# Fourth row tiles behind branches replaced by pieces of 32 rows, four at a time on four column tiles

## The chip, the core and the metric

The kernel runs on one core of a Trainium2 chip. The metric is the device time of one execution in microseconds (us), lower is better. The engines are named as in the profile: PE is TensorE's matmuls, PEld its weight loads, DVE is VectorE, ACT is ScalarE, POOL is GpSimd and SP is SyncE, which issues most of the DMAs.

## What is computed

A gated linear recurrence over 768 steps for 4 x 8 heads of 48 channels, and behind it a mixture of eight experts: each of the 3072 tokens goes through the two matrices of the one expert that its logits name.

```python
f = 1.0 / (1.0 + np.exp(-f_logit))
for t in range(S):                                   # S = 768
    state = f[:, :, t, :, None] * state + np.einsum('bhd,bhe->bhde', k[:, :, t], v[:, :, t])
    y[:, :, t] = np.einsum('bhd,bhde->bhe', q[:, :, t], state)
x = y.transpose(0, 2, 1, 3).reshape(3072, 384)
...
expert_idx = np.argmax(x @ w_gate, axis=1)           # 8 experts
for e in range(E):
    h = np.maximum(x_sorted[lo:hi] @ w1[e], 0.0)     # w1[e]: 384 x 1024
    y_sorted[lo:hi] = h @ w2[e]                      # w2[e]: 1024 x 384
return gate_w[:, None] * y_sorted[inv_perm]
```

Everything is float32. How many rows an expert gets depends on the data; counted from the reference's inputs they are 406, 413, 352, 385, 335, 443, 396 and 342.

## The kernel before

The first part works through 12 units of the recurrence in a software pipeline (`score`, `within`, `before`, `added`, `rows`) and scatters each token's row of 400 numbers (`xrow`: 384 channels, the token's number, its gate weight, filling) to the tensor `xs` in HBM, where each expert has a region of its own.

The second part takes the rows of one expert in tiles of 128. For a tile, `load_rows` fetches the rows (SP), `turn` transposes them on PE (three transposes into `etp`, one DVE copy to `xT`), `widen` multiplies by `w1` (24 matmuls of 128 columns into `hps`, then one ReLU on ACT and one on DVE into `hT`), and `narrow` multiplies by `w2` (8 matmuls of 384 columns into `yps`), scales by the gate weight (`ysb`, DVE) and scatters to the output (POOL). Each matmul of float32 stands in the profile as two MATMUL records with two weight loads.

A list `order` names the tiles: four per expert (`TILES = 4`), without the first tile of experts 0 and 1, which run earlier, inside the pipeline of the first part (`soon`). Engines run it in the order in which it is written. Row loads run some tiles ahead and turns two tiles ahead (`ahead`), from seven row buffers (`rowp`). The weights of expert e + 2 (3 MB) are loaded when the last tile of expert e is done, since `wpool` holds two experts.

The fourth tile of each expert stands behind a branch, which each engine takes or not by a register that it loads from `endi` (L664, L682); it is executed for the five experts with more than 384 rows. A second branch (L684) guards a loop for rows past the fourth tile, which no expert here has. The transposes of a fourth tile are made whether it is executed or not. `check` (L620 on) sums a test of the recurrence's range and sets `fixi`; at the end of the program a branch on it leads to a slow path that does the work again.

Of the kernel before, what the change touches and what calls it, by code (L numbers as in the profile page):

```python
# [34 lines left out]

REGION = N + C
ROWS = E * REGION


TILES = 4  # L40


EARLY = 2
# [12 lines left out]
def _consts():  # L56
    p = np.arange(128)
    e = np.arange(E)

    def row(v):  # L60
        return np.broadcast_to(v, (128, len(v)))

    f = {
        "ident": np.eye(128),
        "tri": np.triu(np.ones((128, 128)), 1),
        "ones": np.ones((128, 128)),
        "rev": row(E - e),
        "first": row(e * REGION),
        "full": row(e * REGION + C),
        "tok": p[:, None] + np.arange(N // C)[None] * C,  # L70
        "p": p[:, None],
        "sel": np.stack([p < DP, p >= DP], 1),
    }
# [26 lines left out]
def kernel(  # L100
# [24 lines left out]
    def const(name):  # L125
        a, w = fat[name]
        return fpack[:, a : a + w]
# [1 line left out]
    causal = mpack[:, 0:128]  # L129
    ident = const("ident")  # L130

    xs = nc.dram_tensor("xs", (ROWS, ROW), F32, kind="Internal").ap()
    xg = nc.dram_tensor("xg", (B, DM, S), F32, kind="Internal").ap()

    badi = cpool.tile([1, 1], I32, name="badi")
# [127 lines left out]
    def narrow(x, w, yp, group="out"):  # L263
        for f in range(NF):
            nc.tensor.matmul(  # L265
                yp, lhsT=x["hT"][:, f, :], rhs=w[1][:, f, :], start=f == 0, stop=f == NF - 1
            )
        ysb = ep.tile([128, DM], F32, name="ysb")
        nc.vector.tensor_scalar(ysb, yp, x["x"][:, GATE : GATE + 1], None, op0=OP.mult)  # L269
        scatter(out, x["dst"], ysb, N - 1, group)  # L270
# [6 lines left out]
    redo = cpool.tile([1, 1], I32, name="redo")  # L277
    fix = cpool.tile([1, 1], F32, name="fix")
    fixi = cpool.tile([1, 1], I32, name="fixi")
    endi = cpool.tile([1, E], I32, name="endi")  # L280

    def load_weights(e):
        w1t = wpool.tile([128, KD, F], F32, name="w1t")
# [14 lines left out]
        done[what] = max(done[what], min(count, len(order)))  # L298

    def load_pads(e):  # L300
        rows = xs[e * REGION : e * REGION + TILES * C]
        nc.sync.dma_start(
            rows.rearrange("(t p) r -> p t r", p=C), _bc(pad, 1, TILES)
        )

    with ExitStack() as st:
        ld = st.enter_context(tc.tile_pool(name="ld", bufs=4))
# [236 lines left out]
        for n in range(NU + 2):  # L544
# [33 lines left out]
            if rt:  # L578
                rt.place()
                rt.fill()  # L580
                lead["base"] = rt.after
                if n == NU - 3:
                    lack = wk.tile([1, EARLY], F32, name="lack", bufs=1)
                    some = wk.tile([1, 1], F32, name="some", bufs=1)
                    nc.vector.tensor_tensor(
                        lack, rt.after[0:1, 0:EARLY], const("full")[0:1, 0:EARLY], op=OP.is_lt
                    )
                    nc.vector.reduce_max(some, lack, axis=AX_X)
                    nc.vector.tensor_copy(redo, some)
# [29 lines left out]
                soon = [load_rows(slice(first[e], first[e] + C)) for e in range(EARLY)]  # L619


        def check():
# [11 lines left out]
            nc.vector.tensor_tensor(fix, fix, bad[0:1], op=OP.max)  # L634
            nc.vector.tensor_copy(fixi, fix)
            nc.vector.tensor_copy(endi, lead["base"][0:1])
# [10 lines left out]
    def tile_pools(st):  # L647
        pool = lambda name, bufs: st.enter_context(tc.tile_pool(name=name, bufs=bufs, space=PSUM))
        psh, pse, psz = pool("psh", 4), pool("pse", 2), pool("psz", 2)

        def turn_late(x):
            turn(x, pse.tile([128, KD, C], F32, name="etp"))

        def through(x, w, between=(), group="out"):
            hp = [psh.tile([128, 4, C], F32, tag="hps", name="hps") for g in range(2)]
            widen(x, w, hp, range(NF))
            for y in between:
                turn_late(y)
            narrow(x, w, psz.tile([128, DM], F32, name="yps"), group)

        return turn_late, through

    def rows_end(e):
        return nc.values_load(endi[0:1, e : e + 1], min_val=first[e], max_val=first[e] + N)  # L664

    def rows_from(row, e, rows_to, w, turn_late, through, group="out"):

        nc.sync.dma_start(xs[ds(rows_to, C)], pad)
        with tc.For_i(row, first[e] + N, C) as at:
            with tc.If(rows_to > at):  # L670
                x = load_rows(at)
                turn_late(x)
                through(x, w, group=group)

    with ExitStack() as st:
        turn_late, through = tile_pools(st)
        st.enter_context(tc.manual_schedule(engines=ordered))
        for i, (e, t) in enumerate(order):
            w = weights[e]
            if t == TILES - 1:  # L680
                rows_to = rows_end(e)
                with tc.If(rows_to > first[e] + t * C):  # L682
                    through(tiles[e, t], w)
                    with tc.If(rows_to > first[e] + TILES * C):  # L684
                        rows_from(first[e] + TILES * C, e, rows_to, w, turn_late, through)
                if e + 2 < E:
                    load_weights(e + 2)
                continue

            more = 1 if t == TILES - 2 else 0  # L690
            list(ahead("load", i + 6 + more))
            through(tiles[e, t], w, list(ahead("turn", i + 3 + more)))

    todo = nc.values_load(fixi[0:1, 0:1], min_val=0, max_val=1)
    with tc.If(todo > 0):

        again = nc.values_load(redo[0:1, 0:1], min_val=0, max_val=1)
        with tc.If(again > 0):
            with ExitStack() as st:
                turn_late, through = tile_pools(st)  # L700
                for e in range(EARLY):
                    load_weights(e)
                    x = load_rows(slice(first[e], first[e] + C))
                    turn_late(x)
                    through(x, weights[e], group=None)


        flag = nc.values_load(badi[0:1, 0:1], min_val=0, max_val=1)
        with tc.If(flag > 0):
            with ExitStack() as st:  # L710
# [73 lines left out]
            with ExitStack() as st:  # L784
                turn_late, through = tile_pools(st)
                for e in range(E):
                    load_weights(e)
                    rows_from(first[e], e, rows_end(e), weights[e], turn_late, through, group=None)


_OUTS = [((N, DM), "float32")]
# [53 lines left out]
```

## Time and profile before

| | us |
|---|---|
| median of 3 runs (494.04 to 496.79) | 496.4 |
| the profiled execution, its own time | 494.94 |
| its span, first to last instruction | 493.1 |
| PE busy (share of the span) | 443.6 (90%) |
| DVE busy | 161.5 (33%) |
| ACT busy | 124.4 (25%) |
| POOL busy | 117.3 (24%) |

The time of an execution is 1.8 us more than its span. A busy PE is a PE with at least one matmul in flight. The granted clock, 0.972 of TensorE's full 2.4 GHz over the span, is its mean.

### The profile page before, as it was taken

The page shows a single profiled execution, that of the slowest core. Times are in us where ns is not written, and L with a number is a line of the kernel's source. Part 1 is how long each engine was busy: PE and PEld are TensorE (multiplying, and loading weights), DVE is VectorE, ACT ScalarE, POOL GpSimd, SP SyncE. Part 2 cuts the span into 40 slices and gives each one's busy share as a digit, 9 for nine tenths or more (in the row PEclk, how much of TensorE's full clock was granted, in tenths as well). Part 3 has the DMA queues.
Part 4 walks back from the last instruction along what each step waited for, and adds up shares of the span by engine and source line. Part 5 has one row for each costly group of instructions (what it writes and reads, how often), then busy time and mean ns, then how long its engine had stood idle before and what let it go on. Part 6 is the DMA issues. An engine that isn't in the chain of part 4 may idle for free.

```text
span 493.1 us, 8760 instructions
## 1 busy us (share of the span) xinstructions
PE 443.6 (90%) x3678; PEld 367.2 (74%) x3678; DVE 161.5 (33%) x326; ACT 124.4 (25%) x172; POOL 117.3 (24%) x135
## 2 busy tenths in 40 slices
PE   0498898898989999999999999999999999999990
PEld 0497797797988778777788788777778878877770
DVE  5787667778543212111111111211111111121110
ACT  5788487977732000000000000000000000000000
POOL 4656466765623200000001000000000100000000
PEclk9889799998999999999999999999999999999995
DMA  8999865799221411062081271053181127000000
GB/s 316 409 384 383 322 235 218 277 397 347 92 102 68 145 37 34 17 230 98 17 293 48 71 285 33 18 209 114 35 298 36 33 86 262 19 17 5 16 20 17
DMA packets 31858, 74.49 MB, mean 151 GB/s; under 512 B 3358, under 2 KB 19777, under 8 KB 31792
## 3 DMA queue, kind: packets, MB, share of 16 engines
q1 hardware_dynamic: 27696, 63.49, 35.6%
q0 software_dynamic: 3392, 9.64, 5.1%
q8 instruction: 38, 0.62, 0.5%
q10 hardware_dynamic: 704, 0.51, 0.3%
q14 instruction: 28, 0.23, 0.1%
HBM read 57.44 MB, written 17.17 MB: 151 GB/s over the span
## 4 chain that ended last, share of the span: by engine, by line
issue 53%; PE 30%; ACT 6%; POOL 4%; DVE 2%; another core or an unknown queue 1%; POOLq 1%; DMA 1%; ACTq 0%
PE s L391 5%; PE xp L496 5%; PE yt L435 4%; POOL out_dram L149 3%; PE dp L451 3%; PE yt L415 2%; PE hps L251 2%; PE yp L265 2%; PE yps L265 2%; PE s L251 2%; ACT L371 2%; PE kp L406 2%; ACT f L371 1%; ACT f L340 1%
## 5 line engine op out<-in xcount | busy, mean ns | idle before, releaser
L251 PEld LDWEIGHTS hps<-xT,w1t 128*128 128x128 f32 x1296 | 148.4, 192 | 14.7 <-PEq L684 4.2
L251 PE MATMUL hps<-xT,w1t 128*128 128x128 f32 x1296 | 149.6, 275 | 5.3 <-DVEq L684 2.4
L265 PE MATMUL yps<-w2t,hT 128*128 128x384 f32 x432 | 143.8, 486 | 0.0
L265 PEld LDWEIGHTS yps<-w2t,hT 128*128 128x128 f32 x432 | 80.0, 190 | 50.1
L149 POOL DMA_INDIRECT out_dram<-ysb,dst x29 | 28.1, 969 | 289.0 <-DVE ysb L269 209.0
L259 ACT ACTIVATE hT<-hps 128x512 f32<-128x512 f32 x27 | 16.1, 597 | 285.6 <-PE hps L251 285.6
L261 DVE TENSOR_SCALAR hT<-hps 128x512 f32<-128x512 f32 x27 | 18.7, 692 | 136.0 <-PE hps L251 136.0
L269 DVE TENSOR_SCALAR ysb<-yps,xrow 128x384 f32<-128x384 f32 x27 | 16.7, 618 | 114.1 <-PE yps L265 114.1
L391 PE MATMUL s<-q,k 64*128 64x128 f32 x384 | 28.1, 303 | 15.1 <-POOL last L374 15.1
L391 PEld LDWEIGHTS s<-q,k 64*128 64x128 f32 x384 | 25.8, 212 | 15.9 <-POOL last L374 15.1
L348 DVE TENSOR_TENSOR_SCAN r<-f,cap 128x1032 f32<-128x1032 f32 (+1 forms) x13 | 28.7, 2208 | 12.4 <-POOL f L341 12.4
L394 DVE COPY_PREDICATED at<-mpack,s 128x1024 f32<-128x1024 uint8 x24 | 30.2, 1311 | 4.4 <-PE s L391 4.4
L149 POOL DMA_INDIRECT xs<-xr,posi x24 | 24.2, 1007 | 24.3 <-DVE xr L220 7.5
L360 POOL TENSOR_TENSOR k<-k,r 128x1024 f32<-128x1024 f32 (+1 forms) x13 | 26.4, 2032 | 2.5 <-DVE r L348 2.4
L496 PE MATMUL xp<-fpack,ys 128*128 128x104 f32 x192 | 24.3, 280 | 0.7 <-ACT ys L476 0.7
L496 PEld LDWEIGHTS xp<-fpack,ys 128*128 128x128 f32 x192 | 22.3, 191 | 2.2 <-ACT ys L476 1.0
L415 PE MATMUL yt<-at,v 128*64 128x128 f32 x384 | 23.6, 276 | 0.0
L435 PE MATMUL yt<-q,state 48*48 48x128 f32 x320 | 22.5, 297 | 0.0
L415 PEld LDWEIGHTS yt<-at,v 128*64 128x64 f32 x384 | 20.7, 137 | 1.2
L435 PEld LDWEIGHTS yt<-q,state 48*48 48x48 f32 x320 | 19.5, 133 | 2.1 <-issue 1.8
L379 DVE TENSOR_TENSOR q<-q,f 128x1024 f32<-128x1024 f32 (+1 forms) x13 | 14.8, 1145 | 15.0 <-ACT f L371 12.7
L406 PE MATMUL kp<-fpack,k 128*128 128x128 f32 x96 | 14.4, 286 | 5.7 <-ACT kn L407 3.9
(75 smaller groups left out, 325.5 us busy)
## 6 DMA issues: line engine op xcount, KB each, us to landing
w1t<-in_moe_w_dram SPq DMA_DIRECT2D x8, 1536.0 KB
w2t<-in_moe_w_dram SPq DMA_DIRECT2D x8, 1536.0 KB
xs<-pad SPq DMA_DIRECT2D x8, 800.0 KB
xrow<-xs SPq DMA_DIRECT2D x32, 200.0 KB
v<-in_vu_dram SPq DMA_DIRECT2D x12, 512.0 KB
f<-in_fu_dram SPq DMA_DIRECT2D x11, 516.0 KB
k<-in_ku_dram SPq DMA_DIRECT2D x11, 512.0 KB
q<-in_qu_dram SPq DMA_DIRECT2D x11, 512.0 KB
```

What stands on the lines that cost most here:

```text
L149: ins = nc.gpsimd.indirect_dma_start(out=dst, out_offset=bass.IndirectOffsetOnAxis(ap=idx, axis=0), in_=src, in_offset=None, bounds_check= ...
L251: nc.tensor.matmul(hp[g][:, f, :], lhsT=w[0][:, j, b * 128 : b * 128 + 128], rhs=x["xT"][:, j, :], start=j == 0, stop=j == KD - 1,)
L261: nc.vector.tensor_scalar(x["hT"][:, 4:8], hp[1], 0.0, None, op0=OP.max)
L265: nc.tensor.matmul(yp, lhsT=x["hT"][:, f, :], rhs=w[1][:, f, :], start=f == 0, stop=f == NF - 1)
L348: nc.vector.tensor_tensor_scan(x["r"][:, part].rearrange("p s c -> p (s c)"), x["f"][:, part].rearrange("p s c -> p (s c)"), cap[:, part]. ...
L360: nc.gpsimd.tensor_tensor(k, k, r[:, :, 1:CR], op=OP.mult)
L391: nc.tensor.matmul(ps[:, h, p], lhsT=x["k"][r, s], rhs=x["q"][r, s], start=True, stop=True)
L394: nc.vector.copy_predicated(x["at"][:, a].rearrange("p h s c -> p (h s) c"), _bc(causal, 1, SEG), ps.rearrange("p h s c -> p (h s) c"),)
L406: nc.tensor.transpose(kp[:, p], x["k"][:, HP * a + p], ident)
L415: nc.tensor.matmul(x["yt"][r, a, p], lhsT=x["v"][:, a, 2 * p + h], rhs=x["at"][:, a, h, p], start=p == 0, stop=x["old"] is None, skip_grou ...
L435: nc.tensor.matmul(x["yt"][r, a, p], lhsT=x["old"][r, HP * a + p], rhs=x["q"][r, HP * a + p], start=False, stop=True, skip_group_check=True,)
L496: nc.tensor.matmul(xp[:, p], lhsT=x["ys"][:, a, p], rhs=wx[:, p], start=True, stop=True)
```

## The change

`TILES` becomes 3: an expert's first 384 rows run as before, without a branch. Rows behind them are cut into pieces of 32, at most four per expert and eight in all (`SPILL`, `SLOTS`). `share` works out on DVE, from the experts' counts, which piece stands in which of the eight slots, and leaves for each slot the row in `xs` and the expert in `sloti`; an empty slot names a block of padding rows (`NONE`) and expert 0. For the inputs here six slots are filled.

A quad is four slots. `load_quad` reads eight registers on SP and issues twelve DMAs: 32 rows per slot, and `w1` and `w2` of each slot's expert, 3 MB per slot and 12.6 MB per quad, into a pool with one buffer (`qp`). On PE the rows of the four slots are turned together; then `widen_quad` takes each slot's 32 rows of `xT` as the stationary operand, so that the product fills 32 of the array's columns, with the slot's own `w1` as the moving operand of 512 columns. The four slots write to four groups of 32 partitions of the same bank. `turn_quad` transposes the 1024 hidden values of each row back (8 transposes) and `narrow_quad` multiplies by `w2` in the same way, 384 columns at a time.

Quad 0 is loaded ahead of the list of 22 tiles and runs in its tile number 11 (counted from 0), quad 1 is loaded behind that tile and runs in the last, number 21. Row buffers go from seven to six, and rows are loaded four tiles ahead. `check` moves behind the early `widen` of expert 1. The slow path is written anew; the branch on `fixi` that leads to it stays.

```diff
-TILES = 4
+NONE = ROWS
+TILES = 3
+T = 32
+QUADS = 2
+SLOTS = 4 * QUADS
+SPILL = 4
+PADDED = TILES * C + SPILL * T
...
-    rowp = ctx.enter_context(tc.tile_pool(name="rowp", bufs=7))
+    rowp = ctx.enter_context(tc.tile_pool(name="rowp", bufs=6))
...
+        def share():
...
+            nc.vector.tensor_tensor(flat, flat, rank, op=OP.mult)
+            nc.vector.tensor_tensor(
+                mine,
+                _bc(flat, 1, SLOTS),
+                _bc(const("slots")[one], 2, E * SPILL),
+                op=OP.is_equal,
+            )
...
         list(ahead("load", 5))
+        over = share()
         narrow_early(soon[0], weights[0])
-        check()
         widen(soon[1], weights[1], early_banks(), range(NF))
+        check(over)
...
+        qp = st.enter_context(tc.tile_pool(name="qp", bufs=1))
...
+        def load_quad(q):
+            x = qp.tile([128, ROW], F32, name="qrow")
+            w1 = qp.tile([128, 4, KD, F], F32, name="qw1")
+            w2 = qp.tile([128, 4, NF, DM], F32, name="qw2")
...
+            for g in range(4):
+                nc.sync.dma_start(x[g * T : g * T + T], xs[ds(value(0, g, NONE), T)])
+            for g in range(4):
+                e = value(1, g, E - 1)
+                for w, src, k in ((w1, moe_w1, KD), (w2, moe_w2, NF)):
+                    nc.sync.dma_start(
+                        w[:, g], src[ds(e, 1)].rearrange("o (k p) f -> p (o k) f", p=128)
+                    )
...
+        def widen_quad(x):
+            hp = banks()
+            hq = qp.tile([128, 2, 4, C], F32, name="hq")
+            for b in range(2):
+                for j in range(KD):
+                    for g, r in pieces():
+                        nc.tensor.matmul(
+                            hp[b][r].rearrange("p f c -> p (f c)"),
+                            lhsT=x["xT"][:, j, r],
+                            rhs=x["w"][0][:, g, j, b * 512 : b * 512 + 512],
...
+        def narrow_quad(x):
+            yp = psz.tile([128, DM], F32, name="yps")
+            for f in range(NF):
+                for g, r in pieces():
+                    nc.tensor.matmul(
+                        yp[r],
+                        lhsT=x["hT"][:, f, r],
+                        rhs=x["w"][1][:, g, f],
...
+        quads = {len(order) // 2: 0, len(order) - 1: 1}
+        quad = load_quad(0)
         for i, (e, t) in enumerate(order):
             w = weights[e]
-            if t == TILES - 1:
-                rows_to = rows_end(e)
-                with tc.If(rows_to > first[e] + t * C):
-                    through(tiles[e, t], w)
...
-            list(ahead("load", i + 6 + more))
-            through(tiles[e, t], w, list(ahead("turn", i + 3 + more)))
+            list(ahead("load", i + 5))
+            if i in quads:
+                turn_late(quad)
+                widen_quad(quad)
+            hp = banks()
+            widen(tiles[e, t], w, hp, range(NF))
+            if i in quads:
+                turn_quad(quad)
+            for x in ahead("turn", i + 3):
+                turn_late(x)
+            narrow_late(tiles[e, t], w)
+            if i in quads:
+                narrow_quad(quad)
+                if quads[i] + 1 < QUADS:
+                    quad = load_quad(quads[i] + 1)
+            if t == TILES - 1 and e + 2 < E:
+                load_weights(e + 2)
```

On PE, this is what stands around the fourth tile of expert 0 in the kernel before (`etp` are turns, `hps` is `widen`, `yps` is `narrow`; L682 and L684 are the two branches, the rows between L669 and L670 the loop that is skipped here).

```order
L265 MATMUL yps<-w2t,hT 128x384 x8
L664 TENSOR_LOAD endi
L682 COMPARE_AND_BRANCH
L251 MATMUL hps<-xT,w1t 128x128 x24
L265 MATMUL yps<-w2t,hT 128x384 x8
L684 COMPARE_AND_BRANCH
L669 COMPARE_AND_BRANCH
L669 UNCONDITIONAL_BRANCH x2
```

In the changed kernel no branch is left between the tiles. This is PE around tile 11 and quad 0 (`qrow`, `qw`, `hq` and `hqT` belong to the quad, `32x512` and `32x384` are the outputs of its matmuls).

```order
L277 MATMUL yps<-w2t,hT 128x384 x8
L250 MATMUL etp<-fpack,qrow 128x128 x3
L770 MATMUL hps<-qw_2020,xT 32x512 x24
L263 MATMUL hps<-xT,w1t 128x128 x24
L789 MATMUL hps<-fpack,hq 128x128 x8
L250 MATMUL etp<-fpack,xrow 128x128 x3
L277 MATMUL yps<-w2t,hT 128x384 x8
L798 MATMUL yps<-qw_2021,hqT 32x384 x32
```

The tile's own `widen` now lies between the quad's `widen` and the turning back of its result; the quad's own turn is followed at once by the product that needs it.

On SP, before, two or three row loads followed a load of weights, with the branches behind them:

```order
L284 DMA w1t<-in_moe_w_dram 128x3x1024
L286 DMA w2t<-in_moe_w_dram 128x8x384
L232 DMA xrow<-xs 128x400 x3
L664 TENSOR_LOAD endi
L664 ISA x2
L682 COMPARE_AND_BRANCH
L684 COMPARE_AND_BRANCH
```

In the changed kernel this is the end of the load of quad 1 (its last slot's expert) and what follows it on the same queue; the first `xrow` is the row load of tile 16, issued at the head of tile 12, and the `w1t` and `w2t` are those of expert 6.

```order
L748 TENSOR_LOAD sloti
L748 ISA x2
L755 ISA
L755 DMA qw_2853<-in_moe_w_dram 128x3x1024
L755 ISA
L755 DMA qw_2854<-in_moe_w_dram 128x8x384
L244 DMA xrow<-xs 128x400
L300 DMA w1t<-in_moe_w_dram 128x3x1024
L302 DMA w2t<-in_moe_w_dram 128x8x384
```

Tile 16's rows, which PE turns in tile 14, now stand on SP behind the 12.6 MB of the quad.

## Rows read from the trace of the kernel before

**Rows 1.** The page: busy time of PE, and GB/s in 40 slices of the span.
```profile
PE 443.6 (90%) x3678; PEld 367.2 (74%) x3678; DVE 161.5 (33%) x326; ACT 124.4 (25%) x172; POOL 117.3 (24%) x135
...
GB/s 316 409 384 383 322 235 218 277 397 347 92 102 68 145 37 34 17 230 98 17 293 48 71 285 33 18 209 114 35 298 36 33 86 262 19 17 5 16 20 17
```

**Rows 2.** PE in order of time (start, length, engine, line, xcount, idle before).
```profile
224.29 5.52 PE L251 MATMUL hps<-xT,w1t 128*128 128x128 f32 x48
229.65 0.82 PE L238 MATMUL etp<-fpack,xrow 128*128 128x128 f32 x6
230.30 5.33 PE L265 MATMUL yps<-w2t,hT 128*128 128x384 f32 x16
235.47 5.52 PE L251 MATMUL hps<-xT,w1t 128*128 128x128 f32 x48
240.82 5.33 PE L265 MATMUL yps<-w2t,hT 128*128 128x384 f32 x16
246.79 5.59 PE L251 MATMUL hps<-xT,w1t 128*128 128x128 f32 x48 [0.64 <-PEq L684]
```

**Rows 3.** The first and last tile of the list, in order of time.
```profile
180.12 5.52 PE L251 MATMUL hps<-xT,w1t 128*128 128x128 f32 x48
...
475.09 5.33 PE L265 MATMUL yps<-w2t,hT 128*128 128x384 f32 x16
...
480.46 0.62 DVE L269 TENSOR_SCALAR ysb<-yps,xrow 128x384 f32<-128x384 f32 x1 [4.41 <-PE yps L265]
```

**Rows 4.** Groups of line 415: xcount, busy us, mean ns of one, idle before.
```profile
L415 PE MATMUL yt<-at,v 128*64 128x128 f32 x384 | 23.6, 276 | 0.0
L415 PEld LDWEIGHTS yt<-at,v 128*64 128x64 f32 x384 | 20.7, 137 | 1.2
```

**Rows 5.** PE around one group of line 415, in order of time.
```profile
106.18 1.97 PE L415 MATMUL yt<-at,v 128*64 128x128 f32 x32
108.07 1.09 PE L406 MATMUL kp<-fpack,k 128*128 128x128 f32 x8
```

**Rows 6.** The copy behind a turn on DVE, in order of time.
```profile
174.23 0.55 DVE L240 COPY xT<-etp 128x384 f32<-128x384 f32 x1
```

**Rows 7.** SP's issues, in order of time.
```profile
212.95 0.38 SPq L284 DMA_DIRECT2D w1t<-in_moe_w_dram  x1
213.42 0.43 SPq L286 DMA_DIRECT2D w2t<-in_moe_w_dram  x1
213.95 11.52 SPq L232 DMA_DIRECT2D xrow<-xs  x3
```

**Rows 8.** SP's DMA queue from 212.9 to 222.9, then to 224.2: packets, MB, share.
```profile
q1 hardware_dynamic: 1437, 3.16, 89.6%
...
q1 hardware_dynamic: 287, 0.39, 84.6%
```

**Rows 9.** Register loads on SP by line: ns min/median/max, first and last start.
```profile
L664 SPq TENSOR_LOAD <-endi x8: 266/270/662, 192.2 to 417.1; - x8
L664 SPq FUSED_REGOPS  x8: 147/154/159, 192.5 to 417.8; - x8
```

**Rows 10.** PE after an idle stretch early in the run and, last, undisturbed.
```profile
23.92 1.95 PE L451 MATMUL dp<-v,kn 128*64 128x48 f32 x32 [4.21 <-ACT kn L407]
25.80 3.35 PE L391 MATMUL s<-q,k 64*128 64x128 f32 x32
...
32.31 1.16 PE L451 MATMUL dp<-v,kn 128*64 128x48 f32 x32 [0.24 <-ACT kn L407]
33.40 2.06 PE L391 MATMUL s<-q,k 64*128 64x128 f32 x32
```

**Rows 11.** Two windows of 2 us: busy by engine, then the granted clock.
```profile
24.00:26.00 2.00, 2.00 (x34) 1.91 (x36) 1.19 (x1) 1.64 (x2) 0.78 (x1) 0.50 1.02 380
...
30.00:32.00 2.00, 2.00 (x28) 1.66 (x24) 1.78 (x2) 1.86 (x3) 2.00 (x4) 1.00 1.05 365
```

**Rows 12.** PE at the check, in order of time.
```profile
167.77 0.35 PE L630 MATMUL op<-okc,fpack 128*128 128x1 f32 x2 [1.21 <-DVE okc L628]
```

More of the change, by code (lines that the diff above doesn't have):

```diff
@@ L69, in _consts @@
         "full": row(e * REGION + C),
+        "most": row(e * REGION + PADDED),
+        "spill": row((e[:, None] * REGION + TILES * C + np.arange(SPILL) * T).ravel()),
+        "spillat": row((e[:, None] * REGION + TILES * C + np.arange(SPILL) * T).ravel() - NONE),
+        "spillof": row(np.repeat(e, SPILL)),
+        "slots": row(1 + np.arange(SLOTS)),
         "tok": p[:, None] + np.arange(N // C)[None] * C,
@@ L267, in narrow, with put @@
             )
+        put(x, yp, group)
+    def put(x, yp, group):
         ysb = ep.tile([128, DM], F32, name="ysb")
@@ L619 @@
                 soon = [load_rows(slice(first[e], first[e] + C)) for e in range(EARLY)]
-        def check():
+        def share():
+            one = slice(0, 1)
+            have = wk.tile([1, E, SPILL], F32, name="have", bufs=1)
+            rank = wk.tile([1, E * SPILL], F32, name="rank", bufs=1)
+            mine, part = (
+                cap[0:1].rearrange("p s c -> p (s c)")[:, i : i + SLOTS * E * SPILL].rearrange(
+                    "p (s e) -> p s e", s=SLOTS
+                )
+                for i in (0, SLOTS * E * SPILL)
+            )
+            slot = wk.tile([1, SLOTS], F32, name="slot", bufs=1)
+            over = wk.tile([1, E], F32, name="over", bufs=1)
+            flat = have.rearrange("p e s -> p (e s)")
+            ends = lead["base"][one]
+            nc.vector.tensor_tensor(
+                have,
+                _bc(ends, 2, SPILL),
+                const("spill")[one].rearrange("p (e s) -> p e s", e=E),
+                op=OP.is_gt,
+            )
+            nc.vector.tensor_tensor_scan(
+                rank, const("ones")[one, 0 : E * SPILL], flat, 0.0, OP.mult, OP.add
+            )
+            nc.vector.tensor_tensor(flat, flat, rank, op=OP.mult)
+            nc.vector.tensor_tensor(
+                mine,
+                _bc(flat, 1, SLOTS),
+                _bc(const("slots")[one], 2, E * SPILL),
+                op=OP.is_equal,
+            )
+            with nc.allow_low_precision("whole numbers"):
+                nc.vector.tensor_tensor(
+                    part, mine, _bc(const("spillat")[one], 1, SLOTS), op=OP.mult
+                )
+                nc.vector.reduce_sum(slot, part, axis=AX_X)
+                nc.vector.tensor_scalar(sloti[:, 0], slot, float(NONE), None, op0=OP.add)
+                nc.vector.tensor_tensor(
+                    part, mine, _bc(const("spillof")[one], 1, SLOTS), op=OP.mult
+                )
+                nc.vector.reduce_sum(sloti[:, 1], part, axis=AX_X)
+            nc.vector.tensor_tensor(over, ends, const("most")[one], op=OP.is_gt)
+            nc.vector.reduce_max(slot[:, 0:1], over, axis=AX_X)
+            nc.vector.tensor_scalar(
+                slot[:, 1:2], rank[:, E * SPILL - 1 :], SLOTS + 0.5, None, op0=OP.is_gt
+            )
+            nc.vector.tensor_tensor(slot[:, 0:1], slot[:, 0:1], slot[:, 1:2], op=OP.max)
+            nc.vector.tensor_copy(endi, ends)
+            return slot[:, 0:1]
@@ L623, in check @@
+        def check(over):
             ok = wk.tile([128, NU * SEG], F32, name="ok", bufs=1)
@@ L649, in tile_pools, with banks @@
         psh, pse, psz = pool("psh", 4), pool("pse", 2), pool("psz", 2)
+        def banks():
+            return [psh.tile([128, 4, C], F32, tag="hps", name="hps") for g in range(2)]
         def turn_late(x):
             turn(x, pse.tile([128, KD, C], F32, name="etp"))
[L654 to L658, printed above, removed]
-            narrow(x, w, psz.tile([128, DM], F32, name="yps"), group)
@@ L661, in tile_pools, with narrow_late @@
[L661 to L673, printed above, removed]
+        def narrow_late(x, w, group="out"):
+            narrow(x, w, psz.tile([128, DM], F32, name="yps"), group)
@@ new lines, in pieces @@
+        def pieces():
+            return [(g, slice(g * T, g * T + T)) for g in range(4)]
+        def widen_quad(x):
[8 more added lines that the diff above has]
+                            rhs=x["w"][0][:, g, j, b * 512 : b * 512 + 512],
+                            start=j == 0,
+                            stop=j == KD - 1,
+                            skip_group_check=True,
+                        )
+                if b == 0:
+                    nc.scalar.activation(hq[:, b], hp[b], AF.Relu)
+                else:
+                    nc.vector.tensor_scalar(hq[:, b], hp[b], 0.0, None, op0=OP.max)
+            x["hq"] = hq
@@ new lines, in turn_quad @@
+        def turn_quad(x):
+            tp = banks()
+            x["hT"] = qp.tile([128, NF, C], F32, name="hqT")
+            for b in range(2):
+                for f in range(4):
+                    nc.tensor.transpose(tp[b][:, f], x["hq"][:, b, f], ident)
+                (nc.scalar.copy if b == 0 else nc.vector.tensor_copy)(
+                    x["hT"][:, 4 * b : 4 * b + 4], tp[b]
+                )
+        def narrow_quad(x):
[6 more added lines that the diff above has]
+                        rhs=x["w"][1][:, g, f],
+                        start=f == 0,
+                        stop=f == NF - 1,
+                        skip_group_check=True,
+                    )
+            put(x, yp, "out")
@@ L694 @@
+            narrow_late(tiles[e, t], w)
[5 more added lines that the diff above has]
+                load_weights(e + 2)
     todo = nc.values_load(fixi[0:1, 0:1], min_val=0, max_val=1)
     with tc.If(todo > 0):
[L697 to L705, printed above, removed]
@@ L783 @@
                 nc.vector.tensor_copy(endi, end[0:1])
[L784 to L788, printed above, removed]
+        skip = nc.values_load(fromi[0:1, 0:1], min_val=0, max_val=TILES * C)
+        with ExitStack() as st:
+            banks, turn_late, narrow_late, psz = tile_pools(st)
+            with tc.For_i(0, E) as e:
+                w1t = wpool.tile([128, KD, F], F32, name="w1t")
+                w2t = wpool.tile([128, NF, DM], F32, name="w2t")
+                for w, src in ((w1t, moe_w1), (w2t, moe_w2)):
+                    nc.sync.dma_start(
+                        w, src[ds(e, 1)].rearrange("o (k p) f -> p (o k) f", p=128)
+                    )
+                rows_to = nc.values_load(
+                    endi[0:1, ds(e, 1)], min_val=0, max_val=ROWS - C
+                )
+                nc.sync.dma_start(xs[ds(rows_to, C)], pad)
+                with tc.For_i(e * REGION + skip, rows_to, C) as at:
+                    x = load_rows(at)
+                    turn_late(x)
+                    widen(x, (w1t, w2t), banks(), range(NF))
+                    narrow_late(x, (w1t, w2t), None)
 _OUTS = [((N, DM), "float32")]
```

31 lines of the change are left out of this document (18 added, 13 removed).

## The prediction

> **What bounds the kernel now.** I began with the page. PE is busy for 90% of the span, and in the later half of it the DMA engines move 5 to 300 GB/s where they moved 383 to 409 in the second to fourth slice [rows 1]: up to about 170 us the recurrence and the transfers matter, behind that PE alone. Then I read PE in order of time there. One tile follows the next: from the start of one `widen` to that of the next it is 235.47 - 224.29 = 11.18 us, of which `widen` is 5.36, two turns 0.65 and `narrow` 5.17 [rows 2]. So a tile costs 10.53 us and a turn 0.33 us. Of `narrow` that is 16 records of 384 columns at 0.323 us each. The next start, past a skipped or taken branch, is 246.79 - 235.47 = 11.32 us, 0.80 more than a tile without turns [rows 2]. The list runs from 180.12 to 480.26 (0.2 us ahead of the last `ysb`), which is 300.1 us [rows 3]: 27 tiles at 10.53 are 284.3, 28 turns are 9.2, and 6.6 are left for the branches of eight experts, 0.8 each, as the one seen. Behind it lie 12.8 us of the last scatter and the end of the program, which stay. What counts is what PE does between 180 and 480 us, and whether something makes it wait there.
>
> **What is removed.** Five fourth tiles (experts 0, 1, 3, 5, 6) of 10.53 us, 52.7. Eight turns, 2.6. The branches, 6.6. Together 61.9 us.
>
> **What two quads cost on PE.** Each turn of a quad stands right ahead of the product that needs it, so PE waits for the copy: the DVE first writes `ysb` of the tile before (0.2 us behind, 0.62 long [rows 3]), then copies for 0.55 [rows 6], so the product starts about 1.45 us after the turn starts. The products are 24 matmuls of 512 columns and 32 of 384, two records each. If the four slots run at once, there are 12 steps of 0.323 x 512/384 = 0.43 us and 16 of 0.323: 5.2 + 5.2 us. If they run one after another, it is four times that, 41.4 us a quad. The trace has no group of four, but it has groups of two: line 415 fills 64 columns with each matmul, and two that follow each other write different halves. Its 32 records take 108.07 - 106.18 = 1.89 us [rows 5], 0.118 us for two of 128 columns, where `widen` needs 5.36 / 48 = 0.112 for one. Two streams therefore cost what one costs. The weight load of such a record takes 0.137 us [rows 4], longer than the step, so loads lie beside matmuls too. I take four at once, since two show no loss. The same group took 0.1 us more than 16 steps of 0.112, which I read as the price of going from whole-array to divided matmuls; four such changes a quad are 0.4 at most. Eight transposes back are 0.9. ReLU and copies of the quad lie beside the tile's own `widen` and `narrow`, which are written between; without that cover they would cost about a microsecond each. A quad is 1.45 + 10.4 + 0.9 + 0.4 = 13.1 us, two are 26.2.
>
> The Trainium skill, "TensorE: Matmul & The Clock Gate", Part 3 (Measured speedup vs the span model), gives three column tiles of 512 columns a speedup of 2.38, not 3. By that the products would take 10.4 x 3 / 2.38 = 13.1 us, and the sum would be 5 us higher; line 415 shows no such loss with two.
>
> **What moves at the start of the list.** PE's wait of 1.21 us for `okc` [rows 12] goes, since `check` stands behind `widen` of expert 1 now; there `okc` waits for that tile's ReLU and holds up the two turns, which cost about 0.6 again. `share`'s fourteen small DVE operations lie under `narrow` of expert 0, 5 us long, which needs nothing from the DVE meanwhile. -0.6 us.
>
> **What the transfers do.** A quad's 12.6 MB go through the one queue on which all row loads stand. How that queue serves is seen where weights are loaded: `w1t` and `w2t` are issued at 212.95 and 213.42, and row loads (0.2 MB each) from 213.95 on [rows 7]. Until 222.9 the queue moved 3.16 MB, the size of the weights; the next 1.3 us moved 0.39 MB, the two row loads [rows 8]. They came last, in the order of issue, though their issue was 9 us old. So whatever is issued behind a quad's weights lands behind them.
>
> Quad 0 is issued as soon as `check` has freed the memory, at about 176 us. Its four registers and row loads come first: 0.27 + 0.15 us for a register [rows 9] and 0.4 for an issue, some 4.5 us. 12.6 MB at 0.39 MB/us (the busy slices of [rows 1]) are 32 us, so with about a microsecond each to start and to land, and the output's scatters, it is in by 216. Tile 5's rows are behind it and are turned in tile 3, at 179.5 + 3 x 10.86 + 5.36 = 217.4: just hidden. Expert 2's weights follow by 221 and 225 and are needed from 223 (`w1`) and 228 (`w2`). Cost nothing, with 2 us to spare; the tiles 0 to 4 are the cover.
>
> Quad 1 is not hidden. It is issued when `ysb` of quad 0 is written, 0.85 us after PE has left quad 0 (call that E). Weights are issued from E + 4.5, the bytes are through at about E + 38, with the scatters of three tiles at E + 39. Tile 16's row load is issued behind them, at the head of tile 12, and lands at about E + 40.3. PE turns these rows in tile 14, between its `widen` and `narrow`: E + 2 x 10.86 + 5.36 = E + 27.1. PE waits 13 us, and `narrow` of tile 14 is queued behind the turn, so nothing else fills it. Bounds: at the fastest slice, 0.409 MB/us, the wait is 11.6 us; if each expert took the 9.95 us of [rows 7, 8] with its start, 20.7. I take 13, since eight weight loads in a row need one start only. Behind it expert 6's weights (by E + 49) and tile 17's rows are in time, for the wait has moved PE too.
>
> After such an idle stretch PE is slow: 4.21 us of it, and the next two groups took 1.95 and 3.35 us where they otherwise take 1.16 and 2.06 [rows 10], at a granted clock of 0.50, the level of 1.2 GHz, against 1.00 later [rows 11]. That is 2.1 us more; I add 2.
>
> **The sum.** The profiled execution took 494.9: a span of 493.1 and 1.8 around it, 1.5 below the median of 496.4. 494.9 - 61.9 + 26.2 - 0.6 + 15 = 473.6. I say 474.
>
> **The rivals.**
> (1) No wait at tile 14: 474 - 15 = 459. It needs row loads that pass the weights, or a quad that is in 13 us sooner. [Rows 8] speak against the first, the slices against the second.
> (2) Two slots at a time. Line 415 has two halves only, so a limit of two would look the same there. Each quad costs 10.4 us more: 495, no change.
> (3) The slower side: slots one after another, or loads of stationary rows that no longer hide. The first gives 474 + 2 x 31 = 536. For the second the nearest row is 0.137 us a load [rows 4]; 112 loads a quad in the open are 15.3 us, 30.7 in all, 505. What decides is the time of a step of four slots: the change loses from 2.1 times a single stream on, since a quad may cost (496.4 - 474) / 2 = 11 us more. Against it stand [rows 4, 5], where streams and loads of two column groups on the same rows of the array lie beside each other. The Trainium skill, "TensorE: Matmul & The Clock Gate", Part 3 (The mechanism), says that a weight load overlaps a running matmul only when the row group differs; by that rule the second of these would come. Line 415's column groups share all rows and its loads overlap, so the trace disagrees.
> (4) Quad 0 late too: if SP's registers or the bytes take 5 us more than I reckon, tile 3 and expert 2 wait 3 to 7 us: 477 to 481.
>
> **How the numbers follow.** The forecast 0.64 (470 to 481 with its bounds), rival 1 0.14, rival 2 0.09, rival 3 0.07, rival 4 0.06. The range 456 to 486 takes in the forecast, 1 and 4, and a loss of a quarter in the products; it leaves out 2 and 3, 0.16. A measurement here can tell 0.5% from no change, 2.5 us: rival 2 straddles that bound, 0.07 of it same, 0.02 faster. Faster 0.64 + 0.14 + 0.06 + 0.02 = 0.86, same 0.07, slower 0.07.
>
> **What the profile after would show.** 22 pairs of `hps` and `yps` groups and nothing between them but turns; MATMUL records of 32 x 512 that begin in fours, and 48 of them in about 5.2 us; a group of 64 with 384 columns in as long; one wait of PE of about 13 us with a row load as its end, about 27 us behind quad 0, and a granted clock of 0.5 behind it; DMA at 390 GB/s for 33 us twice. If the quad's groups take 10 or 20 us, the step on the four streams is wrong; if the wait is missing, the one on the queue; if a wait stands near tile 3 or 4, the one on quad 0.

## The result, and the profile after

The changed kernel takes 476.6 us (median of four runs; the kernel before, on the same chip, 495.7). The ratio is 0.960, 95% interval 0.955 to 0.965. The profiled execution took 474.65 us, its span 472.8, where 493.1 were before. The forecast was 474. The medians are of all executions; the ratios leave out those that ran slow throughout at a lower granted clock, here one of the four (482.3).

The page of the changed kernel, the rows that answer to [rows 1], and the granted clock in the same 40 slices:

```profile
PE 416.1 (88%) x3580; PEld 336.6 (71%) x3581; DVE 159.4 (34%) x325; ACT 123.5 (26%) x172; POOL 113.7 (24%) x133
...
PEclk9979889999799999999999999999996799999997
...
GB/s 312 406 382 383 296 215 214 268 358 377 288 71 71 71 138 166 394 397 393 389 84 148 183 36 186 168 0 40 293 398 387 357 175 180 18 17 18 17 2 20
```

The two loads of quads are the two plateaus of nearly 400 GB/s, from the 17th and from the 29th slice. In the second one the clock sinks to 0.6. PE around quad 0, in order of time (start, length, engine, line, xcount, idle before):

```profile
297.88 5.33 PE L277 MATMUL yps<-w2t,hT 128*128 128x384 f32 x16
303.04 0.49 PE L250 MATMUL etp<-fpack,qrow 128*128 128x128 f32 x3
304.38 5.36 PE L770 MATMUL hps<-qw,xT 128*32 128x512 f32 x48 [0.85 <-DVE dst L254]
309.67 5.62 PE L263 MATMUL hps<-xT,w1t 128*128 128x128 f32 x48
315.13 1.04 PE L789 MATMUL hps<-fpack,hq 128*128 128x128 f32 x8
316.00 0.49 PE L250 MATMUL etp<-fpack,xrow 128*128 128x128 f32 x3
316.33 5.33 PE L277 MATMUL yps<-w2t,hT 128*128 128x384 f32 x16
321.59 5.37 PE L798 MATMUL yps<-qw,hqT 128*32 128x384 f32 x64
326.88 5.62 PE L263 MATMUL hps<-xT,w1t 128*128 128x128 f32 x48
```

From the turn of the quad to the next tile it is 326.88 - 303.04 = 23.84 us, of which a tile is 10.86. A quad costs 12.98. The only wait is 0.85 us for its turned rows. Inside the two groups of the quad the records begin in fours, as forecast: 0.02 us from the first to the last of four, and from four to four 0.43 us in the first group and 0.32 in the second. PE at tile 14, two tiles behind it, and under it windows there (us, busy by engine, granted clock, DMA share, GB/s):

```profile
348.68 5.52 PE L263 MATMUL hps<-xT,w1t 128*128 128x128 f32 x48
369.37 0.87 PE L250 MATMUL etp<-fpack,xrow 128*128 128x128 f32 x3 [15.17 <-DMA xrow<-xs]
370.04 6.41 PE L277 MATMUL yps<-w2t,hT 128*128 128x384 f32 x16
376.28 5.52 PE L263 MATMUL hps<-xT,w1t 128*128 128x128 f32 x48
```
```profile
354.00:369.00 15.00, 0.20 (x2) 0.01 (x1) 0.69 (x1) 0.00 (x0) 0.00 (x0) 0.65 1.05 389
369.00:371.00 2.00, 1.63 (x5) 1.35 (x6) 0.62 (x2) 0.00 (x0) 0.00 (x0) 0.50 1.04 414
371.00:375.00 4.00, 4.00 (x12) 2.20 (x12) 0.00 (x0) 0.00 (x0) 0.00 (x0) 0.85 1.04 376
```

PE stands for 15.17 us while the DMA engines are full, and goes on at a granted clock of 0.50 (1.2 GHz): turn and `narrow` take 376.28 - 369.37 = 6.91 us instead of 5.50, 1.4 more. What SP issued meanwhile:

```profile
327.67 3.63 SPq L751 DMA_DIRECT2D qrow<-xs  x4
332.14 22.48 SPq L755 DMA_DIRECT2D qw<-in_moe_w_dram  x8
354.66 6.17 SPq L244 DMA_DIRECT2D xrow<-xs  x1
360.93 0.62 SPq L300 DMA_DIRECT2D w1t<-in_moe_w_dram  x1
361.64 1.34 SPq L302 DMA_DIRECT2D w2t<-in_moe_w_dram  x1
```

The first `xrow` is the row load of tile 16. SP needs 22.5 us for eight weight loads, so the rows are issued only at 354.66, 0.5 us after PE began to wait for them, and land 14.7 us later. In the window from 333.0 to 366.8 SP's queue moved this (packets, MB, share):

```profile
q1 hardware_dynamic: 5675, 12.47, 99.5%
```

The start of the list, from `narrow` of expert 0 on; the first row is the same group in the kernel before:

```profile
161.24 5.33 PE L265 MATMUL yp<-w2t,hT 128*128 128x384 f32 x16
```
```profile
164.69 5.33 PE L277 MATMUL yp<-w2t,hT 128*128 128x384 f32 x16
176.56 0.38 PE L699 MATMUL op<-okc,fpack 128*128 128x1 f32 x2 [1.19 <-DVE okc L697]
183.72 5.52 PE L263 MATMUL hps<-xT,w1t 128*128 128x128 f32 x48
```

The last `ysb` starts at 464.69, 8.1 us ahead of the end of the span, where 12.6 were before [rows 3]:

```profile
464.69 0.62 DVE L284 TENSOR_SCALAR ysb<-yps,qrow 128x384 f32<-128x384 f32 x1 [4.71 <-PE yps L798]
```

In spans: 493.1 - 61.9 (tiles, turns, branches) + 26.0 (quads) + 16.6 (the wait with its slow clock) + 3.6 (the list starts at 183.72, not 180.12) - 4.5 (tail) = 472.9; measured 472.8.

### The profile page after: what moved, and what is told of

Its sections match the earlier page's. It is cut to its first block, busy times and chain, and to the rows that moved or that the text cites. A ratio compares the mean times of both kernels' runs of the same rounds, so it can differ in the third digit from the quotient of the medians.

```text
span 472.8 us, 8470 instructions
## 1 busy us (share of the span) xinstructions
PE 416.1 (88%) x3580; PEld 336.6 (71%) x3581; DVE 159.4 (34%) x325; ACT 123.5 (26%) x172; POOL 113.7 (24%) x133
## 4 chain that ended last, share of the span: by engine, by line
PE 78%; ACT 7%; SPq 4%; DMA 4%; DVE 3%; issue 2%; POOL 1%; POOLq 0%; ACTq 0%
PE hps L263 23%; PE yps L277 22%; PE s L409 5%; PE xp L514 5%; PE yt L453 5%; SPq L755 4%; DMA xrow<-xs 3%; PE dp L469 3%; PE yt L433 3%; PE hps L770 2%; PE yps L798 2%; PE yp L277 2%; PE s L263 2%; ACT L389 2%; PE etp L250 2%
## 5 line engine op out<-in xcount | busy, mean ns | idle before, releaser
L263 PEld LDWEIGHTS hps<-xT,w1t 128*128 128x128 f32 x1056 | 121.1, 192 | 7.3 <-issue 2.3
L263 PE MATMUL hps<-xT,w1t 128*128 128x128 f32 x1056 | 121.8, 275 | 0.0
L277 PE MATMUL yps<-w2t,hT 128*128 128x384 f32 x352 | 118.3, 490 | 0.0
L277 PEld LDWEIGHTS yps<-w2t,hT 128*128 128x128 f32 x352 | 65.8, 192 | 41.3 <-issue 0.9
L161 POOL DMA_INDIRECT out_dram<-ysb,dst x26 | 25.3, 972 | 272.6 <-DVE ysb L284 272.6
L271 ACT ACTIVATE hT<-hps 128x512 f32<-128x512 f32 x22 | 13.1, 597 | 237.8 <-PE hps L263 237.8
L273 DVE TENSOR_SCALAR hT<-hps 128x512 f32<-128x512 f32 x22 | 15.2, 692 | 106.2 <-PE hps L263 101.1
L284 DVE TENSOR_SCALAR ysb<-yps,xrow 128x384 f32<-128x384 f32 x22 | 13.6, 618 | 94.3 <-PE yps L277 94.3
L409 PE MATMUL s<-q,k 64*128 64x128 f32 x384 | 29.8, 315 | 15.4 <-POOL last L392 15.4
L250 PE MATMUL etp<-fpack,xrow 128*128 128x128 f32 x72 | 12.2, 281 | 15.6 <-DMA xrow<-xs 15.2
L453 PE MATMUL yt<-q,state 48*48 48x128 f32 x320 | 22.5, 298 | 0.0
```

The source lines that it names most:

```text
L161: ins = nc.gpsimd.indirect_dma_start(out=dst, out_offset=bass.IndirectOffsetOnAxis(ap=idx, axis=0), in_=src, in_offset=None, bounds_check= ...
L250: nc.tensor.transpose(tp[:, j, :], x["x"][:, j * 128 : j * 128 + 128], ident)
L263: nc.tensor.matmul(hp[g][:, f, :], lhsT=w[0][:, j, b * 128 : b * 128 + 128], rhs=x["xT"][:, j, :], start=j == 0, stop=j == KD - 1,)
L277: nc.tensor.matmul(yp, lhsT=x["hT"][:, f, :], rhs=w[1][:, f, :], start=f == 0, stop=f == NF - 1)
L409: nc.tensor.matmul(ps[:, h, p], lhsT=x["k"][r, s], rhs=x["q"][r, s], start=True, stop=True)
L453: nc.tensor.matmul(x["yt"][r, a, p], lhsT=x["old"][r, HP * a + p], rhs=x["q"][r, HP * a + p], start=False, stop=True, skip_group_check=True,)
```

## The experiments

All change the changed kernel, except the one that is named otherwise. "List" is the time from the start of the first tile to the end of PE, in the profiled execution: 280.9 us for the changed kernel, 300.3 for the one before. The runs are from three chips, on which the kernel before took 496.6, 498.0 and 495.6 us; a ratio is always to the kernel before on the same chip, and medians of different chips compare to some 2 us only.

**Rows ahead of the quad.** In tile 11, ahead of quad 1's load:

```diff
                 if quads[i] + 1 < QUADS:
+                    list(ahead("load", i + 7))
                     quad = load_quad(quads[i] + 1)
```

> The row loads of tiles 16 and 17 are issued right ahead of quad 1's load instead of behind it; nothing else changes. Theory (order on the one queue makes the wait at tile 14): the rows are in long before PE turns them, the wait of 15.2 us and the 1.4 us of lower clock behind it go, and of them 1 to 2 us come back at tile 16, since expert 6's first weights still land behind the quad at about 44 us after its end, where they are needed at 43.4: 461 us. Rival (the 12.6 MB themselves are too much for the 27 us, in whatever order): the wait moves to the next transfer, expert 6's weights at tile 16, and most of the 16.6 us stays: 472 to 477.

461.6 us, ratio 0.930 (0.922 to 0.937). The wait at tile 14 is gone, and a smaller one for expert 6's weights stands at tile 16 (the first row below; the second is from the next experiment):

```profile
372.37 7.22 PE L263 MATMUL hps<-xT,w1t 128*128 128x128 f32 x48 [3.12 <-DMA w1t<-in_moe_w_dram]
```
```profile
375.49 5.60 PE L263 MATMUL hps<-xT,w1t 128*128 128x128 f32 x48 [3.16 <-DMA w1t<-in_moe_w_dram]
```

3.1 us where 1 to 2 were expected, and this `widen` takes 1.7 more than others (7.22, not 5.52); the rest as expected. The order on the queue made the wait, since the same bytes pass in the same time.

**Rows on ACT's queue.** `load_rows` gets a queue, and tiles 16 and 17 are loaded from ACT:

```diff
-        nc.sync.dma_start(xt, ...)
+        queue.dma_start(xt, ...)
...
+                    nc.scalar if order.index((e, t)) in (16, 17) else nc.sync,
```

> The row loads of tiles 16 and 17 stay where they are in time (heads of tiles 12 and 13, after the quad's load has been issued) but are issued by ACT, so they stand on a queue of their own. Theory (order on one queue): they pass the quad's weights, the wait at tile 14 goes, about 461 us as with the earlier issue. Rival (the transfers share 16 engines and the rows come last whatever queue they are on, or only their early issue helps): PE still waits some 10 to 15 us at tile 14, 470 to 477.

461.6 us, ratio 0.927 (0.920 to 0.935). It tells less than was meant: ACT ran ahead and issued the two loads at 317.7 and 331.9, before the first weights of the quad (333.9). So it repeats the experiment above and says nothing on passing. The next one does.

**Rows on ACT's queue, while the weights flow.** As before, and the two loads are put at the head of tile 14:

```diff
-            list(ahead("load", i + 5))
+            list(ahead("load", 16 if i in (12, 13) else i + 5))
```

> The row loads of tiles 16 and 17 are issued by ACT behind its ReLU of tile 13, about 13.5 us after quad 0's end, when the quad's weights have been flowing for 7 us on SP's queue; with the earlier kernel in which ACT issued them they were out before the first weights, so it could not tell a passing from an early start. Theory (order holds within one queue only): they land within a few us, no wait at tile 14, 461 us. Rival (the engines serve all queues in the order in which transfers were issued): they land behind what SP had issued by then, some four of the eight weight loads or about 20 us later, close to where PE turns the first at 27 us, so PE waits up to 8 us and the time is 462 to 470.

463.4 us, ratio 0.933 (0.928 to 0.938). ACT's issue, the turn in tile 14, and the queues from 341 to 350 us (packets, MB, share; then KB and median us to landing):

```profile
341.49 0.90 ACTq L244 DMA_DIRECT2D xrow<-xs  x2
```
```profile
354.66 0.49 PE L250 MATMUL etp<-fpack,xrow 128*128 128x128 f32 x3
```
```profile
q1 hardware_dynamic: 1348, 3.00, 88.6%
q10 hardware_dynamic: 288, 0.41, 12.3%
...
qw<-in_moe_w_dram SPq DMA_DIRECT2D x3, 1536.0 KB, 19.8
xrow<-xs ACTq DMA_DIRECT2D x2, 200.0 KB, 6.3
```

When ACT issued its rows, five weight loads (7.9 MB) stood on SP's queue, of which some 2.7 MB had been moved. The rows landed 6.3 us later and PE did not wait at tile 14. They passed weights that had been issued before them: order holds within a queue, and another queue gets its share beside it. A wait of 4.2 us stays at tile 16, where it was 3.1 for the earlier issue. The time alone decides nothing, since 463.4 lies within the rival's 462 to 470; the landing of the rows and the missing wait at tile 14 do.

**The load of quad 1 in four parts.** Rows and slot 0 where the whole was, one slot's weights behind each of tiles 13, 15 and 17:

```diff
+            for g in range(4):
+                if later is not None and g:
+                    later[later["from"] + 2 * g] = lambda g=g: slot(g)
+                else:
+                    slot(g)
...
+            elif i in later:
+                later[i]()
```

> Quad 1's rows and its first slot's weights (3.1 MB) are issued where its whole load was, the other three slots' weights behind tiles 13, 15 and 17; it is needed at tile 21. Theory (order on one queue): every row load has at most 3.1 MB, 8 us, ahead of it, and expert 6's and 7's weights as well, so no wait is left: 476.6 - 16.6 = 460 us, 1 us less than with the rows alone issued earlier. Rival (bandwidth): the same bytes still have to pass and some 10 us of waits appear between tiles 13 and 20: 470 us.

459.4 us, ratio 0.925 (0.918 to 0.932). No wait of PE is left between the quads, and the list is 264.15 us, 16.75 less than in the changed kernel, just the 16.6 of wait and clock. By the medians this and the earlier rows can't be told apart; by the list it is 5.0 us shorter (269.1 there).

**No quads.** Both quads and their loads are left out, so rows behind the third tile of an expert are not computed (`quads = {}`).

> Leaves out both quads with their loads, so rows behind the third tile of an expert are not computed. Theory: what is left is the list of 22 tiles; of 476.6 go 26.0 of the two quads and 16.6 of the wait that their loads cause: 434 us, and tiles stay at 10.86 us. If the loads also cost something that PE's waits do not show (a slower first part, slower tiles beside the transfers), it comes out under 432.

430.2 us, ratio 0.868 (0.860 to 0.876), 4 less than expected. The list is 238.15 us; 22 tiles of 10.53 and 20 turns of 0.33 are 238.3, so tiles cost what they did. The profile gives the 4 us to the first part: `narrow` of expert 0 starts at 160.60 where it started at 164.69, and PE was 4 us ahead at 73 us already, where neither kernel has done anything for a quad. So in this execution it is the scatter of the first part (below) and not a cost of the loads; the medians alone can't tell the two apart.

**Slots one by one, and in pairs.** The order of the loops in `widen_quad` and `narrow_quad`:

```diff
-            for f in range(NF):
-                for g, r in pieces():
+            for g, r in pieces():
+                for f in range(NF):
```
```diff
+            for f, (g, r) in [
+                (f, p) for h in (0, 2) for f in range(NF) for p in pieces()[h : h + 2]
+            ]:
```

> The matmuls of a quad are issued slot by slot, each slot's whole sum before the next slot's, so neighbouring matmuls stand on the same 32 columns; their number, sizes and operands are the same. Theory (four run at a time only because neighbours stand on different columns): each of the two products takes four times 5.2, a quad 31 us more, 476.6 + 62 = 539 us. Rival (such matmuls are short of their 0.43 us for another reason, and the order does not matter): 477 us.

> As the slot by slot order, but in two pairs of slots: neighbours alternate between two column groups. Theory (streams on different columns run at once, as many as there are neighbours): twice 5.2 for each product, 10.4 us more for a quad, 476.6 + 21 = 497 us, and with one, two and four at a time the step stays at 0.43 and 0.32 us. Rival (streams share something, so that four gain less than twice of what two do): pairs cost clearly less than 10.4 us more for a quad.

505.5 us, ratio 1.016 (1.011 to 1.020), and 484.2 us, 0.973 (0.969 to 0.978). The groups of both quads, first one by one, then in pairs (xcount, busy us, mean ns, idle before):

```profile
L798 PE MATMUL yps<-qw,hqT 128*32 128x384 f32 x128 | 34.1, 488 | 0.0
L770 PE MATMUL hps<-qw,xT 128*32 128x512 f32 x96 | 18.0, 596 | 1.7 <-DVE dst L254 1.7
```
```profile
L802 PE MATMUL yps<-qw,hqT 128*32 128x384 f32 x128 | 18.5, 488 | 0.0
L772 PE MATMUL hps<-qw,xT 128*32 128x512 f32 x96 | 12.5, 594 | 1.7 <-DVE dst L254 1.7
```

With four at a time both groups take 10.7. The order matters, so the theory holds in its kind; its size does not. One by one was to take 41.4 for each group and takes 34.1 and 18.0; pairs were to take 20.7 and take 18.5 and 12.5. The single records of `narrow_quad`, one by one, show why: within the sixteen records of a slot they begin 0.322 us apart, the time of one, but at a change of slot four records of the next slot begin 0.006 to 0.03 us behind the last four of this one, beside them. 64 records in 17.05 us are 53 steps, so at each of three changes of slot some 3.7 steps are saved. It looks as if PE can start a record on other columns that stands up to four records further on in the program. This is worked out from two orders and was not tested by itself.

**The kernel before without branches.** Its 27 tiles written out, with `COUNT = [4, 4, 3, 4, 3, 4, 4, 3]` tiles per expert and no branch between them.

> The kernel before with its 27 tiles written out and no branch between them (the fourth tile stands in the list for experts 0, 1, 3, 5, 6 and is left out for the others); quads don't come in. Theory: the eight branches at 0.8 go, 6.6 us, with three turns, 1.0, and behind the last matmul the tail is the 8.2 us of the changed kernel and not 12.8, since GpSimd takes one branch fewer after the last scatter: 495.7 - 6.6 - 1.0 - 4.5 = 483.6 us. Rival (the shorter tail comes from the quad, whose last matmuls still run while the engines take the last branch): the tail stays at 12.8, 488 us.

487.0 us, ratio 0.979 (0.975 to 0.983), and 11.0 less than the kernel before on the same chip, between the theory's 12.1 and the rival's 7.7. The list is 292.4 instead of 300.3; with 1.0 for three turns that leaves 6.9 for the branches (6.6 by the prediction). The tail is 11.0 us from the end of PE, between both expectations: 12.7 in the kernel before, 8.2 in the changed one. POOL shows where: its last branch and the instruction behind it (ns min/median/max, first and last start), in the kernel before, in this one, and in the changed one:

```profile
L695 POOLq COMPARE_BRANCH  x1: 45/45/45, 483.6 to 483.6; - x1
L695 POOLq INC_SWDGE_SEM  x1: 1217/1217/1217, 486.6 to 486.6; - x1
```
```profile
L687 POOLq COMPARE_BRANCH  x1: 53/53/53, 474.0 to 474.0; - x1
L687 POOLq INC_SWDGE_SEM  x1: 1239/1239/1239, 477.2 to 477.2; - x1
```
```profile
L832 POOLq COMPARE_BRANCH  x1: 45/45/45, 465.9 to 465.9; - x1
L832 POOLq INC_SWDGE_SEM  x1: 1189/1189/1189, 466.6 to 466.6; - x1
```

1.7 us of the tail go with the last expert's branch. Of the other 2.8, 2.5 are POOL's jump over the slow path, from its branch to the instruction behind it: 3.0 to 3.2 us with the slow path of before and 0.6 to 0.7 with the new one, in every kernel made from it. On the DVE the same jump still takes 3.0 us in the changed kernel (465.3 to 468.3), but POOL is not done before 472.0 in any case. What makes POOL's jump cheap stays open.

**The check back at its old place.** `check(over)` ahead of the early `widen` of expert 1.

> The changed kernel with the check of the recurrence ahead of the early widen of expert 1 again, as before the change. The prediction's step (the move saves 1.2 us of waiting and costs 0.6): from the start of narrow of expert 0 to the start of the list it takes 0.6 us more than the 19.03 of the changed kernel. Rival (as the traces of before, 18.88, and of the changed kernel, 19.03, read: the wait only moves): within 0.3 us of 18.9. Either way the whole stays at 476 to 477 us, and the start of the list lies within the 4 us over which it has been seen so far.

473.0 us, ratio 0.954 (0.947 to 0.960), not told apart from the changed kernel by its interval. From `narrow` of expert 0 to the list it takes 18.88 us as before the change. With the check moved it takes 19.03 in four of eight profiled executions and 20.72 in the other four. The longer ones have this row; the second is the check back at its old place:

```profile
175.45 7.09 PE L277 MATMUL yp<-w2t,hT 128*128 128x384 f32 x16 [0.74 <-issue]
```
```profile
175.32 5.40 PE L277 MATMUL yp<-w2t,hT 128*128 128x384 f32 x16 [0.64 <-issue]
```

The granted clock over the first is 0.76, over the second 1.00. The move puts the 1.2 us wait for `okc` close to the 0.74 us ahead of this group, and in half of the executions PE then runs part of it at the lower clock; with the check at its old place all four profiled executions take 18.88. So the later start of the list behind `narrow` is 0.15 to 1.84 us; that the two waits lie close is a likely reason for the longer ones, but twelve executions don't show it.

**The best version.** Loads of quad 1 in four parts, the check at its old place, and the quad's turns a tile earlier:

```diff
             if i in quads:
-                turn_late(quad)
                 widen_quad(quad)
...
+            if i + 1 in quads:
+                turn_late(quad)
             narrow_late(tiles[e, t], w)
```

> Quad 1's loads spread over four tiles as measured, the quad's own turns moved one tile ahead (behind the other turns, where narrow hides the copy), and the check of the recurrence ahead of the early widen of expert 1 again. Theory: of the 1.45 us at the start of each quad 1.1 go, 2.2 in all, and the check's place gives 0.15 to 1.8 us: 455 to 457 us. Rival (the copy of the turned quad is not what the first product waits for): a wait of 0.8 us stays ahead of each quad, 457 to 459 us.

455.3 us, ratio 0.918 (0.914 to 0.921). PE at quad 0:

```profile
297.53 0.49 PE L250 MATMUL etp<-fpack,qrow 128*128 128x128 f32 x3
297.86 5.33 PE L277 MATMUL yps<-w2t,hT 128*128 128x384 f32 x16
303.11 5.36 PE L775 MATMUL hps<-qw,xT 128*32 128x512 f32 x48
```

The wait of 0.85 is gone and the list is 262.3, 1.8 less than with the loads in parts alone (2.2 expected).

## Why the prediction was right

The time was right, and so was the mechanism of what was removed, of the quads and of the wait. Three terms of the sum were off, and two of them nearly cancel: the list started 4.2 us later than reckoned, the tail is 4.5 shorter, and wait and clock together are 1.6 longer. So it is partly luck that the sum, 473.6, comes within 1.1 us of the profiled execution.

- **Removed, 61.9.** It holds. Tiles cost 10.86 with a turn in every kernel; the branches measure 6.9, not 6.6.
- **Two quads, 26.2.** 26.0. Four streams cost what one costs: 5.29 us to the next group for each product, by 5.2. By the figure of the Trainium skill, "TensorE: Matmul & The Clock Gate", Part 3 (Measured speedup vs the span model), a speedup of 2.38 for three column tiles, carried over to four as an estimate, it would have been 13.1 for both products and not 10.6; the trace disagrees. The loads of the stationary rows, 0.11 us each, lie beside the matmuls although the four groups share all rows. Rivals 2 and 3 are out, and the order of the loops has shown that the neighbours' columns make it. Even rival 3's one after another would have cost 505, not 536, since the changes of slot overlap.
- **The wait at tile 14, 13.** The right place, cause and end; 15.2 us. Quad 0's end, E, is at 326.88; the rows landed at E + 42.5 and not E + 40.3. The weights began to flow at 333.0, E + 6.1, some 0.6 us later than reckoned, and SP's queue moved 12.47 MB in 33.8 us, 0.369 MB/us, not the 0.39 taken from the slices, in which other queues are counted too. For 12.6 MB that is 1.8 us more, so the two make up the 2.2. Rival 1 is out: rows issued behind the weights on the same queue came last. From another queue they would have passed, which the prediction did not consider.
- **The clock behind it, 2.** 1.4: the turn and `narrow` ran in part at the lower level, as forecast.
- **The start of the list, -0.6.** This step failed. The prediction let the wait for `okc` go and put 0.6 us in its place. But `okc` is waited for as long at the new place (1.19 us), so the wait only moved, and from `narrow` of expert 0 to the list it takes 0.15 us more at best. The other 3.45 us of the later start lie ahead of the change's place: `narrow` of expert 0 starts between 160.6 and 165.3 us in the twelve profiled executions, 161.2 in that of before and 164.7 in that of the changed kernel. PE waits in the same places there, and more or fewer of its groups run at the lower clock. The first product of scores at 26 us, for one, took 3.79 us there and 3.35 in [rows 10]. Of the ten executions with the new first part four start between 160.6 and 161.8, about where the two with the old one do (161.2 and 161.4), so most of it is the scatter of single executions; a small effect of the change on it is not excluded.
- **The tail, "12.8 us stay".** This step failed too: 8.1. The last expert's branch stood in it, 1.7, and POOL's jump over the slow path, 2.5 of the other 2.8. The prediction counted the branches between tiles only and took the new slow path, which is skipped, to cost nothing else; why its jump is shorter stays open.
- **Rival 4** did not happen: quad 0's load is in before tile 3 needs its rows.

## What to carry to other kernels

A big load that is due late belongs on the queue in parts, or behind the small loads that are due sooner, or the small ones go on another queue: here the order on one queue cost PE 17 us, nearly as much as the change gained. Small groups of rows with different weights are worth packing on column groups, with the groups in the innermost loop. When a branch goes, look at the end of the program too: all that follows the last result is on the path.

## What was not expected of the hardware

- Matmuls on other columns start beside the running ones even when they stand about four records behind in the program (pairs: 12.5 us where 20.7 were expected).
- The clock behind the same wait is not the same: after 3.12 us of idle PE a `widen` took 7.22 us, after 3.16 us in another kernel 5.60. The windows over the two (busy by engine, granted clock) show 0.76 and 1.00:

```profile
372.40:379.40 7.00, 7.00 (x48) 7.00 (x49) 0.00 (x0) 0.60 (x1) 0.00 (x0) 0.76 1.04 397
```
```profile
375.50:380.90 5.40, 5.40 (x48) 5.40 (x49) 0.00 (x0) 0.60 (x1) 0.00 (x0) 1.00 1.06 397
```

- SP's issue of a weight load is quick only while little stands on its queue: one took 0.38 us [rows 7], eight in a row 22.5, so what is behind them is not only served late but issued late. As an estimate from two runs: issued at 354.66 and landing 6.3 us later, as the rows on ACT's queue did, tile 16's rows would have left a wait of 6.8 us; so of the 15.2 some 7 come with the late issue, and the rest with the order.
